# A layer with attention and a dense branch: five and three maxima in the two steps of a chunk of seven products

## The chip, the cores and the metric

The kernel runs on one core of a Trainium2 chip. The metric is the device time of one execution in microseconds (us).

## The reference

The input x has 2048 rows of 512 numbers. Each row is normalized (xn). Then two branches are computed from xn and joined:

```
q = xn @ wq  (32 heads of 16),  k = xn @ wk,  v = xn @ wv   (one head of k and v for all)
p = softmax(q . k / 4)  over all 2048 keys
s = (p @ v, heads side by side) @ wo
h = xn @ w1 + b1            (1792 wide)
g = silu( (h * tanh(softplus(h))) @ w2 )
out = x + s * g
```

Everything is float32, and the softmax subtracts the maximum of a row's scores.

## The kernel before

**Steps.** The queries are worked off in 32 units (`NU`): four blocks of 512 queries, each with eight units of four heads. A unit has 16 steps, one for each 128 keys, so there are 512 steps. In a step TensorE makes four score tiles of 128 keys by 512 queries (`e_one`, line 1030), ScalarE takes their exponentials (line 1032), and two steps later TensorE multiplies them with v (`pv`, line 1104). The maxima that the softmax subtracts belong to later units and run ahead: a step holds four more score products, turned the other way (128 queries by 512 keys, `m_one`, line 1050), and VectorE takes the maximum along each row (line 1054). Once a unit's maxima are complete, `c_rows` turns them into rows of the query tile. All of this is an order written out in the program: instructions reach the engines in the order of emission, and each engine works in that order.

**Dense products.** Between scores and maxima the program puts the products of the dense work: wq, w1, w2 and wo, each value split into a high and a low part so that a product is three matmuls. A group is one tile of 128 by 512 that is summed in the bank `xps`, of which there is one. The groups of the first two thirds of w2 (`m2_groups`, `THIRDS`) have 15 matmuls, those of the last third, wq, w1 and wo have 12. `chunk_size` cuts a group into chunks of at most eight (`XMAX`): 15 becomes 8 and 7, 12 becomes 6 and 6. A chunk takes two steps: each of its matmuls is made as two halves of 64 rows (`half`), in the first step with one half of the TensorE rows, in the second (`second`) with the other. A group ends with the second step of its last chunk; `finish` then has the bank read out, by a copy on ScalarE (first third of w2, line 839; w1, line 770; wq) or by an addition or multiplication on VectorE (`dve` is set; w2's second and last third at line 845, wo).

**Waves.** Scores and maxima contract over at most 64 rows as well, so a step has two sides that run beside each other: the side of the products (`h`), and the other one (`1 - h`). `em(k)` hands out the maxima to the two sides, after the pattern `EM` = "MEMEMEME" (M a maximum, E a score). `m_sides` gives `k // 2` of the four maxima to the side of the scores and the rest to the side of the products, and keeps the two sides within `MLAG` of each other. `waves` (line 634) then emits the two sides in turn: a product, one entry of the other side, the next product and so on. One such pair is called a wave here. With eight products the sides are 8 products, and 4 scores + 4 maxima; with seven they are 7 products + 1 maximum, and 4 scores + 3 maxima; with six, 6 + 1 and 4 + 3. After the waves of a step come the products with v.

**Banks and waits.** Scores rotate through three banks (`ps_e`, tag "e"), maxima through three others (`ps_m`, tag "m"). Between the two steps of a chunk there is a further wait: the first product of the second step waits for the `relay`, the exponential or maximum of an entry emitted with or behind the last product of the first step, because both halves sum in one bank. Where a group ends and VectorE reads its bank, the maxima emitted from the moment when `HOLD` products are left are held back (`held`) and put behind the reading.

The last 20 steps (`LEAD`) have no maxima any more and are emitted by another function, and a lead of some 94 us ahead of the steps follows a planner. Neither has chunks of seven that the change touches.

Of the kernel before, what the change touches and what calls it, by code (L numbers as in the profile page):

```python
# [32 lines left out]
NU = 8 * NC  # L33
# [9 lines left out]
HOLD = 1  # L43
# [4 lines left out]
MLAG = 4  # L48
# [76 lines left out]
def block_kernel(ctx: ExitStack, tc: tile.TileContext, x, wq, wk, wv, wo, w1, b1, w2, out):  # L125
# [3 lines left out]
    ps_e = ctx.enter_context(tc.tile_pool(name="ps_e", bufs=3, space=bass.MemoryType.PSUM))  # L129
    ps_m = ctx.enter_context(tc.tile_pool(name="ps_m", bufs=3, space=bass.MemoryType.PSUM))  # L130
# [8 lines left out]
    lead = {}  # L139
# [140 lines left out]
    xp_of = {}  # L280
# [209 lines left out]
    cur = {"g": None, "ps": None, "n": 0, "chunk": [], "relay": None}  # L490
# [10 lines left out]
    def begin():  # L501
        prepare()
        if qqueue and is_ready(qqueue[0]):
            g = qqueue.popleft()
        elif queue and is_ready(queue[0]):
            g = queue.popleft()
        else:
            n = next((n for n, g in enumerate(queue) if g.wo is None), None)
            if not n or not is_ready(queue[n]) or queue[n].m1 is None:
                return False  # L510
            g = queue[n]
            del queue[n]
        if g.start:
            g.start()
        if g.alloc:
            ps = g.alloc()
        else:
            ps = ps_x.tile([P, 512], F32, tag="x", name="xps")
        cur.update(g=g, n=0, ps=ps, chunk=[], relay=None)
        return True  # L520

    def finish():
        g = cur["g"]
        if cur["n"] < len(g.mms):
            return False
        for i in g.items:
            i.users -= 1
        cur["g"] = None
        evacs[0] += g.dve
        if lead:  # L530
            lead["post"](g, cur["ps"])
        else:
            g.post(cur["ps"])
            g.done = step[0]
        return True
# [95 lines left out]
    def chunk_size(n):  # L631
        return -(-n // -(-n // XMAX)) if n else 0

    def waves(h, em, new):

        if not cur["chunk"] and (not new or cur["g"] is None and not begin()):
            mms = []  # L640
        else:
            g = cur["g"]
            mms = cur["chunk"] or g.mms[cur["n"]:cur["n"] + chunk_size(len(g.mms) - cur["n"])]
        second = bool(cur["chunk"])
        k = len(mms)
        ms = em(k)
        a = deque(ms[1 - h])
        b = deque(ms[h])
        ps = cur["ps"]
        ends = second and cur["n"] + k == len(cur["g"].mms)  # L650
        xs = deque(mms)
        relay = None
        first = True
        done = False
        while a or b or xs:
            if xs:
                i = xs.popleft().half(ps, h)
                if first and cur["relay"] is not None:
                    tc.add_manual_dep(i.ins, cur["relay"].ins.name, mybir.DependencyInfo(
                        mybir.DependencyClass.Sync, mybir.DependencyReason.DATA), reason="other half of the bank")  # L660
                first = False
                if ends and cur["g"].dve and len(xs) == HOLD:
                    held[0] = []
                if not xs and ends:
                    cur["n"] += k
                    cur["chunk"] = []
                    finish()
                    done = True
                    for top in held[0] or ():
                        top()  # L670
                    held[0] = None
            elif b:
                b.popleft()()
            if len(a) > 1 or a and not xs:
                r = a.popleft()()
                if k and not xs and relay is None:
                    relay = r
        if k and not done:
            assert relay is not None
            cur["relay"] = relay  # L680
            if second:
                cur["n"] += k
                cur["chunk"] = []
            else:
                cur["chunk"] = mms
# [308 lines left out]
    for c in range(NC):  # L994
        for k in range(3):
            a = take(2)
# [38 lines left out]

    m_next = [0, 0]

    def m_one(a):
        v, n = MSEQ[m_next[a]] if m_next[a] < 64 else divmod(m_next[a], 32)
        m_next[a] += 1  # L1040
        if v not in mb_of:
            mb_of[v] = sb.tile([P, 4, 16], F32, tag="mb", name=f"mb{v}", bufs=2)
        q = qt_of[v]
        kb, j = divmod(n, 8)
        p, t = divmod(j, 4)
        o = 64 * a
        ps, tag = (ps_e, "e") if lead and 15 in xp_of and a else (ps_m, "m")
        m = ps.tile([P, C], F32, tag=tag, name=f"m{v}_{a}_{n}")
        o = slice(o, o + (HALF if v < len(qts) else 48))
        pe.matmul(m, q[o, p, P * t:P * (t + 1)], ks[o, C * kb:C * (kb + 1)], start=True, stop=True)  # L1050
        z = 8 * a + 4 * p + t

        def top():
            return dve.reduce_max(out=mb_of[v][:, kb, z:z + 1], in_=m, axis=AX.X)  # L1054
        if held[0] is None:
            return top()
        held[0].append(top)

    def m_sides(h, n):

        ahead = m_next[h] - m_next[1 - h]
        lo = max((4 - MLAG - ahead + 1) // 2, 4 - (32 * NU - m_next[1 - h]))
        hi = min((4 + MLAG - ahead) // 2, 32 * NU - m_next[h])
        return max(min(n, hi), lo)

    def c_rows(v):

# [203 lines left out]
    for c0, c1 in ((0, 1), (1, 2), (2, 3), (3, 4)):  # L1271
# [4 lines left out]
        for c in range(c0, c1):  # L1276
            xs, scs = [], []
            for t in range(4 * c, 4 * c + 4):
# [3 lines left out]
                if c == 0:  # L1282
                    hi = task("ACT", 0.55, lambda t=t: x_high(t), [tr])
                    lo = task("DVE", 0.65, lambda t=t: x_low(t), [hi])
# [5 lines left out]
                else:  # L1290
                    lo = task("ACT", 0.62, lambda t=t: x_copy(t), [tr])
# [65 lines left out]
    while True:  # L1357
# [7 lines left out]
        b = best("PE")  # L1365
        m = m_ready(T["PE"])
        if m is not None and b and b[0] < T["PE"] + 0.2 and T["DVE"] > T["PE"] + 1.0:
            m = None
# [10 lines left out]
        s, e, k = min(opts, key=lambda o: o[0])  # L1379
# [5 lines left out]
        if k == "M":  # L1385
# [7 lines left out]
            if vdone[0] == 0 and min(m_next) >= m_need(0):  # L1393
                vdone[0] = 1
                r = c_rows(0)
# [18 lines left out]
        elif k == "J":  # L1414
            tag = next((g for g in ("wq", "ws", "wb") if (g == "wq" or s > 19.0) and arrived(g) and busy[0] + E0 < s + 0.5), None)
            n = ran[0]
# [16 lines left out]
    while left:  # L1433
        k = next(k for k in left if all(d.end is not None for d in k.deps))
# [18 lines left out]
    for s in range(NS + 2000):  # L1453
        inm = s < NS - LEAD
        if inm or cur["chunk"]:
            assert s < NS
            due(s)
            h = s % 2

            def em(k):  # L1460
                n = m_sides(1 - h, k // 2) if inm else 0
                x = deque(lambda i=i: e_one(s, i) for i in range(4))
                y = deque(lambda: m_one(1 - h) for _ in range(n))
                r = [[], []]
                for op in EM:
                    if op == "M" and y:
                        r[1 - h].append(y.popleft())
                    elif op == "E":
                        r[1 - h].append(x.popleft())
                r[h] = [lambda: m_one(h) for _ in range(4 - n if inm else 0)]  # L1470
                return r

            if s >= 2 and (s - 1) % 16 == 0 and s > 1:
                gap[0] += 1
            waves(h, em, inm)
            act_jobs(1 + (len(jobs) > 2))
            due(s + 0.5)
            pv_to(s - 2)
        elif s < NS:
            due(s)  # L1480
            if not late_banks:
                late_banks.extend(ps_m.tile([P, C], F32, tag="m", name=f"late{k}") for k in range(3))
                if (NS - s) % 2:
                    for i in range(4):
                        e_one(s, i)
                    fill(4)
                    act_jobs(1)
                    pv_to(s - 2)
                    step[0] = s
                    continue  # L1490
            if (NS - s) % 2 == 0:
                late_pair(s)
            else:
                act_jobs(1)
                pv_to(s - 1)
        else:
            due(s)
            pv_to(NS - 1)
            act_jobs(100)
            lanes_end()  # L1500
            due(s + 0.5)
            fill(16)
        step[0] = s
        if vdone[0] < 8 * NC and min(m_next) >= m_need(vdone[0]):
            r = c_rows(vdone[0])
            rowq.extend([r[0], lambda r=r: (r[1](), r[2](), r[3]())])
            vdone[0] += 1
        if rowq and not evacs[0]:
            rowq.popleft()()
        evacs[0] = 0  # L1510
        pump()
        if s > NS + 1 and not queue and cur["g"] is None and not timed and not jobs:
            break
# [12 lines left out]
```

## Time and profile before

| | us |
|---|---|
| median of 3 runs | 1590.27 (1589.85 to 1590.56) |
| profiled execution | 1596.07 |
| span of the profiled execution | 1594.3 |

| engine | busy, us | share of the span |
|---|---|---|
| TensorE (matmuls) | 1579.1 | 99% |
| TensorE (weight loads) | 842.3 | 53% |
| VectorE | 1346.8 | 84% |
| ScalarE | 1306.9 | 82% |
| GpSimd | 629.4 | 39% |

In the rows of the profile PE is TensorE's matmuls, PEld its weight loads, DVE VectorE, ACT ScalarE, POOL GpSimd, SP the queue that issues DMAs. A row of the timeline gives the start and the duration in us, the engine, the line, the operation, and what is written and read: `e` is a score bank, `m` a bank of a maximum, `xps` the bank of the dense sum, `pt` an exponential, `mb` the maxima, `pv` the product with v. Behind them stands in brackets how long the engine sat idle, and what ended that. xN says that N neighbouring instructions are merged in one row. A step begins with the load of its first product, which is the `xps` load with some 0.84 us of idle time ahead of it (the loads of the products with v are through early).

### The profile page before, as it was taken

How to read it: one execution, taken by the hardware profiler on the slowest of the kernel's cores; microseconds unless marked ns; L12 is line 12 of the kernel's file. 1: busy time of each engine (PE TensorE's matmuls, PEld its weight loads, DVE VectorE, ACT ScalarE, POOL GpSimd, SP SyncE). 2: the span in 40 equal slices, each digit the busy share in tenths (PEclk: the TensorE clock that was granted, in tenths of full speed). 3: DMA queues.
4: the chain of work that ended last, by engine and by line, in shares of the span. 5: the costliest groups of instructions: out<-in, count | busy, mean ns of one | idle time of the engine just before them, and what ended most of it. 6: DMA issues, size and time to landing. Idle time of an engine off the chain costs nothing.

```text
span 1594.3 us, 31628 instructions
## 1 busy us (share of the span) xinstructions
PE 1579.1 (99%) x11708; PEld 842.3 (53%) x11708; DVE 1346.8 (84%) x2335; ACT 1306.9 (82%) x2515; POOL 629.4 (39%) x643
## 2 busy tenths in 40 slices
PE   9999999999999999999999999999999999999998
PEld 5455555555555455555555555555555555555554
DVE  8888888888989888888898988888889998888832
ACT  7478788798898778978989787897898878789876
POOL 3477166265464104613425221362252414226413
PEclk9899999999999999999999999999999999999999
DMA  6233131142331304112122321220332213031020
GB/s 193 93 103 124 41 111 50 44 137 84 94 118 35 112 18 150 58 52 82 37 67 86 86 82 44 96 70 18 123 97 84 67 59 97 17 110 58 9 87 28
DMA packets 74666, 124.31 MB, mean 78 GB/s; under 512 B 21520, under 2 KB 35344, under 8 KB 74512
## 3 DMA queue, kind: packets, MB, share of 16 engines
q1 hardware_dynamic: 74512, 122.29, 24.7%
q8 instruction: 93, 1.52, 0.4%
q14 instruction: 61, 0.50, 0.1%
HBM read 74.78 MB, written 26.21 MB: 63 GB/s over the span
## 4 chain that ended last, share of the span: by engine, by line
PE 96%; DVE 2%; ACT 1%; DMA 1%; SPq 0%; issue 0%; POOL 0%; DVEq 0%
PE xps L118 46%; PE pv L1104 32%; PE m L1050 8%; PE e L1030 6%; PE xps L114 1%; DVE mb L1054 1%; PE kp L319 1%; ACT pt L1032 0%; DMA wbs<-w 0%; PE late L118 0%; DMA xin<-in_dram 0%; PE xp L287 0%; PE late L1030 0%; PE wop L118 0%; DVE xt L162 0%
## 5 line engine op out<-in xcount | busy, mean ns | idle before, releaser
L1054 DVE TENSOR_REDUCE mb<-m 128x1 f32<-128x512 f32 x2048 | 1271.4, 682 | 178.1 <-PE m L1050 142.0
L1032 ACT ACTIVATE pt<-e 128x512 f32<-128x512 f32 x2019 | 1061.7, 602 | 227.9 <-PE e L1030 222.0
L1050 PE MATMUL m<-ks,qt 48*128 48x512 f32 (+1 forms) x2048 | 847.9, 424 | 2.1 <-DVE ks L237 1.1
L1030 PE MATMUL e<-qt,ks 64*128 64x512 f32 x2019 | 736.5, 401 | 1.0 <-ACT pt L1032 1.0
L1104 PE MATMUL pv<-pt,vaug 128*32 128x512 f32 x4096 | 543.2, 604 | 0.0
L1050 PEld LDWEIGHTS m<-ks,qt 48*128 48x128 f32 (+1 forms) x2048 | 373.9, 186 | 65.4 <-DVE mb L1054 31.8
L1030 PEld LDWEIGHTS e<-qt,ks 64*128 64x128 f32 x2019 | 372.8, 186 | 15.9 <-ACT pt L1032 8.5
L118 PE MATMUL xps<-wbs,act 64*128 64x512 f32 x1240 | 336.2, 407 | 1.3 <-DMA wbs<-w 1.3
L118 PEld LDWEIGHTS xps<-wbs,act 64*128 64x128 f32 x1240 | 216.1, 185 | 177.4 <-ACT pt L1032 105.7
L118 PE MATMUL xps<-xt,ws 64*128 64x512 f32 x1104 | 305.8, 410 | 0.3 <-DVE y L845 0.3
L118 PEld LDWEIGHTS xps<-xt,ws 64*128 64x128 f32 x1104 | 190.2, 185 | 182.8 <-ACT pt L1032 121.6
L172 POOL TENSOR_SCALAR t<-t 128x512 f32<-128x512 f32 x56 | 34.5, 616 | 326.8 <-ACT t L778 326.5
L1104 PEld LDWEIGHTS pv<-pt,vaug 128*32 128x32 f32 x4096 | 81.7, 108 | 143.9 <-issue 134.7
L162 POOL TENSOR_TENSOR hb<-hb,t 128x512 f32<-128x512 f32 x56 | 72.2, 1289 | 68.3 <-ACT t L791 46.8
L118 PE MATMUL xps<-xt,wq 64*128 64x512 f32 x336 | 93.1, 410 | 0.0
L118 PEld LDWEIGHTS xps<-xt,wq 64*128 64x128 f32 x336 | 57.9, 185 | 55.6 <-ACT pt L1032 35.2
L118 PE MATMUL xps<-wbs,ot_all 64*128 64x512 f32 x288 | 79.5, 408 | 0.0
L118 PEld LDWEIGHTS xps<-wbs,ot_all 64*128 64x128 f32 x288 | 49.5, 184 | 47.0 <-ACT pt L1032 31.9
L162 POOL TENSOR_TENSOR hb<-hb,u 128x512 f32<-128x512 f32 x56 | 72.3, 1291 | 4.4
L162 POOL TENSOR_TENSOR u<-u,t 128x512 f32<-128x512 f32 x56 | 71.8, 1282 | 4.7
L162 POOL TENSOR_TENSOR act<-hb,act 128x512 fp32r<-128x512 f32 x55 | 70.8, 1288 | 4.6
L162 POOL TENSOR_TENSOR oc<-oc,sc 128x512 f32<-128x512 f32 (+1 forms) x16 | 20.6, 1287 | 120.7 <-ACT sc L1132 52.9
(144 smaller groups left out, 955.5 us busy)
## 6 DMA issues: line engine op xcount, KB each, us to landing
wbs<-w SPq DMA_DIRECT2D x36, 512.0 KB
ws<-w SPq DMA_DIRECT2D x35, 512.0 KB
qt<-qh SPq DMA_DIRECT2D x256, 32.0 KB
wq<-wq SPq DMA_DIRECT2D x14, 512.0 KB
w<-wbs SPq DMA_DIRECT2D x14, 512.0 KB
wbs<-wo SPq DMA_DIRECT2D x12, 512.0 KB
rawws<-in_dram SPq DMA_DIRECT2D x21, 256.0 KB
rawwb<-in_dram SPq DMA_DIRECT2D x20, 256.0 KB
```

What stands on the lines that cost most here:

```text
L114: return self.pe.matmul(ps, self.lhs(), self.rhs(), start=(self.k == 0), stop=(self.k == self.tot - 1))
L118: i = self.pe.matmul(ps, self.lhs()[o], self.rhs()[o], start=(self.k == 0 and self.halves == 0), stop=(self.k == self.tot - 1 and self.hal ...
L162: eng.tensor_tensor(out=o, in0=a, in1=b, op=op)
L172: pool.tensor_scalar(o, o, lim, 0.0, op0=ALU.min, op1=ALU.max)
L319: pe.matmul(kp_of[c], wkf[:, dt], xf_of[c][dt // 2][:, dt % 2], start=(dt == 0), stop=(dt == 3))
L1030: pe.matmul(e, ks[o:o + 64, P * k:P * (k + 1)], q[o:o + 64, p], start=True, stop=True)
L1032: r = act.activation(pt, e, AF.Exp, scale=0.25)
L1050: pe.matmul(m, q[o, p, P * t:P * (t + 1)], ks[o, C * kb:C * (kb + 1)], start=True, stop=True)
L1054: return dve.reduce_max(out=mb_of[v][:, kb, z:z + 1], in_=m, axis=AX.X)
L1104: pe.matmul(o[32 * j:32 * j + 32], vaug[:, k], pt, start=(k == 0), stop=(k == 15))
```

## The change

It touches only steps whose chunk has an odd number of products, which are those of seven. The two steps of such a chunk have eight maxima together, before and after. Before they are four and four, after it five and three (`tot` in `m_sides`). In the first step the side of the scores gets four maxima and four scores, and the side of the products its seven products and, as the last thing of the step (`swap`), the fifth maximum; that one is put into a score bank (`other`), behind the fourth score. The relay of that step is the fourth exponential. In the second step the side of the scores has four scores and three maxima, and the side of the products has its seven products alone. Where VectorE reads the bank at the end of the group, maxima are held back from the moment when two products are left, not one (`HOLD + k % 2`).

```diff
@@ waves
-        ms = em(k)
+        ms = em(k, second)
...
+        swap = k % 2 and not second
...
-                if ends and cur["g"].dve and len(xs) == HOLD:
+                if ends and cur["g"].dve and len(xs) == HOLD + k % 2:
                     held[0] = []
...
-            elif b:
+            elif b and not swap:
                 b.popleft()()
             if len(a) > 1 or a and not xs:
                 r = a.popleft()()
-                if k and not xs and relay is None:
+                if k and not xs and relay is None and not (swap and a):
                     relay = r
+            if b and swap and not xs and not a:
+                b.popleft()()
@@ m_one
-    def m_one(a):
+    def m_one(a, other=False):
...
-        ps, tag = (ps_e, "e") if lead and 15 in xp_of and a else (ps_m, "m")
+        ps, tag = (ps_e, "e") if other or lead and 15 in xp_of and a else (ps_m, "m")
@@ m_sides
-    def m_sides(h, n):
-
+    def m_sides(h, k, second):
+
+        tot = 4 + (0 if k % 2 == 0 else -1 if second else 1)
+        tot = min(tot, 64 * NU - sum(m_next))
         ahead = m_next[h] - m_next[1 - h]
-        lo = max((4 - MLAG - ahead + 1) // 2, 4 - (32 * NU - m_next[1 - h]))
-        hi = min((4 + MLAG - ahead) // 2, 32 * NU - m_next[h])
-        return max(min(n, hi), lo)
+        lo = max((tot - MLAG - ahead + 1) // 2, tot - (32 * NU - m_next[1 - h]), 0)
+        hi = min((tot + MLAG - ahead) // 2, 32 * NU - m_next[h], tot)
+        n = max(min((k + tot - 4) // 2 if k % 2 else k // 2, hi), lo)
+        return n, tot - n
@@ em
-            def em(k):
-                n = m_sides(1 - h, k // 2) if inm else 0
+            def em(k, second):
+                n, rest = m_sides(1 - h, k, second) if inm else (0, 0)
...
-                r[h] = [lambda: m_one(h) for _ in range(4 - n if inm else 0)]
+                r[h] = [lambda j=j: m_one(h, n + rest > 4 and j == rest - 1) for j in range(rest)]
```

## The prediction

> **What bounds the kernel now.** I read the page's busy shares, then its chain and its groups, and after that the timeline of single engines, one step at a time.
>
> ```profile
> span 1594.3 us, 31628 instructions
> PE 1579.1 (99%) x11708; PEld 842.3 (53%) x11708; DVE 1346.8 (84%) x2335; ACT 1306.9 (82%) x2515; POOL 629.4 (39%) x643
> PE 96%; DVE 2%; ACT 1%; DMA 1%; SPq 0%; issue 0%; POOL 0%; DVEq 0%
> L1054 DVE TENSOR_REDUCE mb<-m 128x1 f32<-128x512 f32 x2048 | 1271.4, 682 | 178.1 <-PE m L1050 142.0
> ```
>
> TensorE is busy 99% of the span and is 96% of the chain; VectorE, which reads the maxima, has idle time before them. So a step lasts as long as its matmuls take, unless one of them waits for a bank. The weight loads show the order inside a step best, because a load carries the wait for its bank. Here is a pair of steps with seven products, first and second:
>
> ```profile
> 1095.03 0.18 PEld L118 LDWEIGHTS xps<-wbs,act 64*128 64x128 f32 x1 [0.84 <-ACT pt L1032]
> ...
> 1096.31 0.18 PEld L118 LDWEIGHTS xps<-wbs,act 64*128 64x128 f32 x1
> 1096.46 0.18 PEld L1030 LDWEIGHTS e<-qt,ks 64*128 64x128 f32 x1
> 1096.55 0.18 PEld L1050 LDWEIGHTS m<-ks,qt 48*128 48x128 f32 x1
> 1097.09 0.16 PEld L1104 LDWEIGHTS pv<-pt,vaug 128*32 128x32 f32 x8 [0.36 <-issue]
> 1098.09 0.18 PEld L118 LDWEIGHTS xps<-wbs,act 64*128 64x128 f32 x1 [0.84 <-ACT pt L1032]
> ...
> 1101.19 0.18 PEld L118 LDWEIGHTS xps<-xt,wq 64*128 64x128 f32 x1 [0.89 <-DVE y L845]
> ```
>
> The first step runs from 1095.03 to 1098.09, 3.05 us, the second to 1101.19, 3.10 us. In each, the seven products on one half of the rows stand beside four scores and three maxima on the other half; the fourth maximum (1096.55) is alone in an eighth wave. A step with six products has only seven waves:
>
> ```profile
> 1106.91 0.18 PEld L118 LDWEIGHTS xps<-xt,wq 64*128 64x128 f32 x1 [0.84 <-ACT pt L1032]
> 1109.76 0.18 PEld L118 LDWEIGHTS xps<-xt,wq 64*128 64x128 f32 x1 [0.84 <-ACT pt L1032]
> ```
>
> That is 2.85 us, so a wave less is worth 0.20 us. This is what the change is after: fifteen waves in a pair, not sixteen. Reading all step starts I find 31 such pairs before the closing steps. 16 end with ScalarE's copy of the sum, 15 with VectorE's addition.
>
> **The second step, with three maxima.** The lone maximum goes, and seven waves are left, 2.85 us. Whether the next group can begin then depends on when its only bank, xps, has been read out.
>
> ```profile
> L839 ACT ACTIVATE y<-xps x16: 603/603/617, 142.6 to 1402.7; 128x512 f32<-128x512 f32 x16
> ```
>
> ```profile
> 1376.64 0.18 PEld L118 LDWEIGHTS xps<-wbs,act 64*128 64x128 f32 x1 [0.84 <-ACT pt L1032]
> ...
> 1379.69 0.18 PEld L118 LDWEIGHTS xps<-xt,wq 64*128 64x128 f32 x1 [0.84 <-ACT y L839]
> ```
>
> ```profile
> 1378.92 0.60 ACT L839 ACTIVATE y<-xps 128x512 f32<-128x512 f32 x1
> ```
>
> ScalarE's copy stands behind the third exponential in its queue and ends at 1379.52, 2.88 us into the step. So far that was hidden, as the step lasted 3.05. With seven waves the next product is due at 2.85 and must wait for the copy, and with 0.05 us for the release (the price is read below) begins at 2.93. The gain is 0.12 us, not 0.20, in 16 pairs: -1.9 us.
>
> ```profile
> 1098.65 1.89 DVE L1054 TENSOR_REDUCE mb<-m 128x1 f32<-128x512 f32 x3 [0.57 <-PE m L1050]
> 1100.45 0.68 DVE L845 TENSOR_TENSOR y<-xps,y 128x512 f32<-128x512 f32 x1
> 1101.05 1.37 DVE L1054 TENSOR_REDUCE mb<-m 128x1 f32<-128x512 f32 x2
> ```
>
> Where VectorE adds, the addition follows three maxima and ends at 1101.13, and the next product began 0.06 later. The change holds the third maximum back too (HOLD + 1), so the addition follows two. It can begin when the seventh product is through, 1.90 us into the step and a few hundredths on, and ends near 2.65, before 2.85 us. The full 0.25 us is gained in 15 pairs: -3.8 us. The held maximum then ends near 3.25, 0.4 into the next step, while VectorE idles for the first 0.57 of a step. If that cover were gone, the next first maximum would slip by the overrun, and a bank of the three with it.
>
> **The first step, with five maxima.** Products and scores now fill eight waves as in a step with eight products, so the count of waves stays. The new element is the fifth maximum in wave eight, behind the fourth score, on the ring of three score banks. The trace of before has no maximum on a score bank in a step, but it shows the ring: the fourth score needs the bank of the first.
>
> ```profile
> 1095.81 0.60 ACT L1032 ACTIVATE pt<-e 128x512 f32<-128x512 f32 x1 [0.95 <-PE e L1030]
> ```
>
> ```profile
> 1096.34 0.60 ACT L1032 ACTIVATE pt<-e 128x512 f32<-128x512 f32 x1
> ```
>
> The first exponential ends at 1096.41 and the fourth score's load starts at 1096.46: 0.05 us from release to load. By the same ring the fifth maximum needs the bank of the second score, whose exponential (1096.34) ends only at 1096.94, 1.91 us into the step. Its load should start near 1.51, as the lone maximum's did (1096.55), to be in time for wave eight. It will start at 1.96 instead, and behind it on TensorE's queue stand the context products (pv) and then the whole second step. What such a late last matmul costs is shown by a step with six products whose fourth score was late:
>
> ```profile
> 241.08 0.61 ACT L1032 ACTIVATE pt<-e 128x512 f32<-128x512 f32 x1
> ```
>
> ```profile
> 241.74 0.18 PEld L1030 LDWEIGHTS e<-qt,ks 64*128 64x128 f32 x1 [0.17 <-ACT pt L1032]
> 242.17 0.16 PEld L1104 LDWEIGHTS pv<-pt,vaug 128*32 128x32 f32 x8 [0.25 <-issue]
> 243.17 0.18 PEld L118 LDWEIGHTS xps<-xt,early 64*128 64x128 f32 x1 [0.84 <-ACT pt L1032]
> ```
>
> From the end of the exponential (241.69) to the next step's first product are 1.48 us. So the first step becomes 1.91 + 1.48 = 3.38 us, 0.33 more than now. In about a third of the 31 first steps the second exponential ends earlier, as here:
>
> ```profile
> 1082.77 0.18 PEld L118 LDWEIGHTS xps<-wbs,act 64*128 64x128 f32 x1 [0.84 <-ACT pt L1032]
> ```
>
> ```profile
> 1084.04 0.59 ACT L1032 ACTIVATE pt<-e 128x512 f32<-128x512 f32 x1
> ```
>
> It ends 1.86 us in, and the loss is 0.29. I take 0.32 as the mean, with bounds of 0.29 and 0.35. One of the 31 costs nothing:
>
> ```profile
> 553.77 0.49 PE L118 MATMUL xps<-wbs,act 64*128 64x512 f32 x1
> ...
> 556.25 0.50 PE L118 MATMUL xps<-wbs,act 64*128 64x512 f32 x1 [1.27 <-DMA wbs<-w]
> ```
>
> There weights come late, and the second exponential is long over before wave eight. That leaves 30 x 0.32 = +9.6 us.
>
> [...] The row: in the late case the load and its matmul begin together, and the matmul's record is longer than the usual 0.39.
>
> ```profile
> 241.74 0.50 PE L1030 MATMUL e<-qt,ks 64*128 64x512 f32 x1
> 242.17 0.64 PE L1104 MATMUL pv<-pt,vaug 128*32 128x512 f32 x4
> ```
>
> About 0.11 us of weight load is thus exposed, which is inside the 1.48. [...]
>
> **VectorE and the rest.** Five maxima fit:
>
> ```profile
> 1361.92 2.48 DVE L1054 TENSOR_REDUCE mb<-m 128x1 f32<-128x512 f32 x4 [0.59 <-PE m L1050]
> ```
>
> Four take 2.48 us, 0.62 each, and this step began at 1361.35: the fourth ends 3.05 in, the fifth 3.67, which is 0.3 into a second step that starts at 3.38. Its first maximum needs VectorE at 0.57; the third score, which takes the fifth maximum's bank, is due past 1.0. Both are covered, so I cost them at nothing. The relay (the first product of the second step waits for the fourth exponential, now a wave later) is covered as well: that exponential ends near 2.9. No DMA and no GpSimd instruction moves, and the maxima of a pair stay eight, so the row constants come due in the same steps.
>
> **Sum.** +9.6 - 1.9 - 3.8 = +3.9 us. The profiled execution took 1596.07 us around its span of 1594.3, the median of the runs is 1590.27; I add 3.9 to each: 1600.0 and 1594.2. With 0.29 to 0.35 us in the first step and 0.10 to 0.20 where ScalarE copies, the forecast alone goes from +1.7 to +5.1, 1592.0 to 1595.4.
>
> **Rivals.** (a) The bank is free in time and the fifth maximum costs nothing; the pairs then give back 5.7 us: 1584.6, faster. The deciding point is in wave eight of the first step: with 30 first steps against 5.7 us, the break-even loss is 0.19, so the second exponential would have to end by 1.77 us, and for the full gain by 1.46. For it speaks that ScalarE has idle time; against it that the earliest end I found is 1.86, set by the score's own wave and not by a queue. Chance 0.09.
> (b) The exposed load is hidden: 30 x 0.21 = 6.3 less 5.7, +0.6 us, 1590.9, no change. [...] Chance 0.05.
> (c) The change does not do in the second step what it says: VectorE's addition still comes behind three maxima, the next product begins at 3.10 as now, and only the copies' 1.9 us are gained: +7.7, 1598.0. For it speaks that held maxima are counted by hand; against it that the fifth product lies just ahead of the third maximum in the order. Chance 0.10.
>
> **How the numbers follow.** The forecast keeps 0.76. About 0.2% (3.2 us) is what a measurement of this kernel can tell from no change. The forecast's 3.9 stands only 0.7 above it, so I put 0.55 of its 0.76 above and 0.21 within. With (c) slower is 0.65, with (b) same is 0.26, faster 0.09. The range reaches from (b) to (c), 1590.8 to 1598.0, and leaves out (a) and thin tails.
>
> **What would show it.** In the profile after: first steps of 3.34 to 3.38 us, with the last L1050 load of the step ended by ACT pt near 1.96 us; second steps of 2.93 us ended by ACT y and of 2.85 where VectorE adds; the total idle time that L1050's loads spend on ScalarE's exponentials rising from about nothing to some 30 x 0.25 us (1.96 less the 1.70 at which the fourth score's load is through). I am wrong if the first steps stay at 3.05 us (a), or if the second steps with an addition stay above 3.0 (c).

## The result, and the profile after

Over 21 runs each, the median went from 1590.9 to 1595.6 us. The ratio of the changed kernel to the one before is 1.0024, 95% interval [1.0015, 1.0033]: some 3.8 us more (2.4 to 5.2 by the interval), slower, as forecast. The two medians lie 4.7 us apart, because a run's time also moves with its lead, which took 88.1 to 94.1 us in the profiled executions (last section).

The page of the kernel after shows almost nothing of it. TensorE is as full as before, and the span of this one execution is even shorter than that of before:

```profile
span 1592.2 us, 31628 instructions
PE 1576.9 (99%) x11708; PEld 841.0 (53%) x11708; DVE 1347.2 (85%) x2335; ACT 1306.6 (82%) x2515; POOL 629.0 (40%) x643
```

So the steps have to be cut out of the span. The two fences below are from the timelines of the weight loads, before and then after: the first step behind the lead, and the step after the last pair of seven.

```profile
94.11 0.18 PEld L118 LDWEIGHTS xps<-xt,early 64*128 64x128 f32 x1 [0.84 <-ACT pt L1032]
...
1520.88 0.18 PEld L118 LDWEIGHTS xps<-wbs,act 64*128 64x128 f32 x1 [0.89 <-DVE y L845]
```

```profile
88.54 0.18 PEld L118 LDWEIGHTS xps<-xt,early 64*128 64x128 f32 x1 [0.84 <-ACT pt L1035]
...
1518.79 0.18 PEld L118 LDWEIGHTS xps<-wbs,act 64*128 64x128 f32 x1 [0.84 <-DVE y L848]
```

Between them lie 1426.77 us before and 1430.25 after: the steps take 3.5 us more. The lead, which the change does not touch, took 5.6 us less in this execution; the last section says why.

Here is the pair that was shown of before, in the kernel after (its lines 1053 and 1033 are the maxima and scores that stood at 1050 and 1030; 1035, 842, 848 and 1057 were 1032, 839, 845 and 1054):

```profile
1091.86 0.18 PEld L118 LDWEIGHTS xps<-wbs,act 64*128 64x128 f32 x1 [0.84 <-ACT pt L1035]
...
1093.39 0.19 PEld L1033 LDWEIGHTS e<-qt,ks 64*128 64x128 f32 x1
1093.82 0.18 PEld L1053 LDWEIGHTS m<-ks,qt 48*128 48x128 f32 x1 [0.24 <-ACT pt L1035]
1094.24 0.16 PEld L1110 LDWEIGHTS pv<-pt,vaug 128*32 128x32 f32 x8 [0.24 <-issue]
1095.24 0.18 PEld L118 LDWEIGHTS xps<-wbs,act 64*128 64x128 f32 x1 [0.84 <-ACT pt L1035]
...
1098.09 0.18 PEld L118 LDWEIGHTS xps<-xt,wq 64*128 64x128 f32 x1 [0.84 <-DVE y L848]
```

The fifth maximum's load comes at 1093.82, 1.96 us into the step, after idle time that ScalarE ended. The first step lasts 3.38 us where it lasted 3.05, the second 2.85 where it lasted 3.10. ScalarE's timeline has the exponential it waited for, the second score's:

```profile
1093.17 0.60 ACT L1035 ACTIVATE pt<-e 128x512 f32<-128x512 f32 x1
```

It ends at 1093.77, and the load follows 0.05 us later. The list of waits (engine, line, what was waited for: us in total, times, longest) has, next to the maxima's waits for VectorE, a line for this that the list of before lacks, the second one here:

```profile
PEld m L1053 <- DVE mb L1057: 29.5, 78, 0.8
PEld m L1053 <- ACT pt L1035: 6.7, 29, 0.3
```

Second steps that end with ScalarE's copy, such as this one, take 2.94 us, and the idle time ahead of the next product is 0.93 us, above the 0.84 that stands ahead of the other steps shown here:

```profile
1374.31 0.18 PEld L118 LDWEIGHTS xps<-wbs,act 64*128 64x128 f32 x1 [0.84 <-ACT pt L1035]
...
1377.25 0.18 PEld L118 LDWEIGHTS xps<-xt,wq 64*128 64x128 f32 x1 [0.93 <-ACT y L842]
```

In second steps that end with VectorE's addition, the addition now follows two maxima. This is VectorE in the second step of the pair above:

```profile
1095.81 1.29 DVE L1057 TENSOR_REDUCE mb<-m 128x1 f32<-128x512 f32 x2 [0.30 <-PE xps L118]
1097.28 0.69 DVE L848 TENSOR_TENSOR y<-xps,y 128x512 f32<-128x512 f32 x1 [0.18 <-PE e L1033]
1097.89 0.68 DVE L1057 TENSOR_REDUCE mb<-m 128x1 f32<-128x512 f32 x1
```

From all step starts, read out in this way, come the figures of this table: the median length of the steps of seven, in us, and how the steps together (between the two starts above) stand to the kernel before.

| kernel | first steps (31) | second, copy (16) | second, addition (15) | all steps, against before |
|---|---|---|---|---|
| before | 3.05 | 3.05 | 3.10 | |
| after | 3.37 | 2.94 | 2.85 | +3.5 |
| e1, fifth on a bank of the maxima | 3.33 | 2.94 | 2.85 | +2.2 |
| e2, hold as before | 3.38 | 2.94 | 3.11 | +7.8 |
| e3, half of the second exponential | 3.16 | 2.93 | 2.85 | +9.2 (see there) |
| e4, first step begins with a score | 3.14 | 2.93 | 2.85 | -2.2 |
| e5, both steps begin with a score | 3.15 | 2.83 | 2.83 | -4.3 |
| e6, as e4, fifth on a bank of the maxima | 3.57 | 2.94 | 2.85 | +9.9 |

Steps of six and of eight products kept their medians (2.85 and 3.07 us before) within 0.01 us in all of these kernels.

### The profile page after: what moved, and what is told of

The parts are those of the page before. It is cut to its first block, busy times and chain, and to the rows that moved or that the text cites. A ratio compares the mean times of both kernels' runs of the same rounds, so it can differ in the third digit from the quotient of the medians.

```text
span 1592.2 us, 31628 instructions
## 1 busy us (share of the span) xinstructions
PE 1576.9 (99%) x11708; PEld 841.0 (53%) x11708; DVE 1347.2 (85%) x2335; ACT 1306.6 (82%) x2515; POOL 629.0 (40%) x643
## 4 chain that ended last, share of the span: by engine, by line
PE 96%; DVE 2%; ACT 1%; DMA 0%; issue 0%; POOL 0%; SPq 0%; DVEq 0%
PE xps L118 45%; PE pv L1110 32%; PE m L1053 8%; PE e L1033 8%; PE xps L114 1%; PE kp L319 1%; DVE mb L1057 1%; ACT pt L1035 1%; PE warm L1261 1%; DMA wbs<-w 0%; PE xp L287 0%; PE wop L118 0%; PE late L118 0%; PE late L1033 0%; DVE xt L162 0%
```

## The experiments

The theory: the first step lasts 1.48 us from the moment at which the bank of its last matmul comes free, and that is when the second score's exponential ends. The rivals: VectorE, with five maxima, sets that step; or the taking of a score bank costs by itself, through the scores behind it; or the relay (the fourth exponential) sets the start of the second step. Each edit is against the kernel after, unless it says otherwise. The kernels e1, e2, e3 and e6 were run once, and their step lengths are what is compared; e4 and e5 were timed as well.

**e1: another ring for the fifth maximum.**

```diff
-        ps, tag = (ps_e, "e") if other or lead and 15 in xp_of and a else (ps_m, "m")
+        ps, tag = (ps_e, "e") if lead and 15 in xp_of and a else (ps_m, "m")
```

> The fifth maximum takes a bank of the maxima's ring, so it needs the bank of the second maximum instead of the second score. Theory (the first step lasts 1.48 us from the release of the bank that the last matmul needs): VectorE has read the second maximum 1.85 us into the step in the changed kernel, so the first steps take 3.33 us, 0.04 less than there (3.37), now ended by VectorE; the rest stays, about 1.1 us less in all. Rival 1 (VectorE's load of five maxima sets the first step): same first steps, 3.37. Rival 2 (taking a score bank is what costs, through the scores behind it): first steps fall to 3.05.

The pair's first step in the timeline of the weight loads:

```profile
1095.60 0.18 PEld L118 LDWEIGHTS xps<-wbs,act 64*128 64x128 f32 x1 [0.84 <-ACT pt L1035]
...
1097.51 0.18 PEld L1053 LDWEIGHTS m<-ks,qt 48*128 48x128 f32 x1 [0.20 <-DVE mb L1057]
...
1098.93 0.18 PEld L118 LDWEIGHTS xps<-wbs,act 64*128 64x128 f32 x1 [0.84 <-ACT pt L1035]
```

3.33 us, and the load now waits for VectorE; all steps together are 1.3 us shorter than in the kernel after, where 1.1 were expected. The wait follows the bank. With the score banks free of the fifth maximum the step did not return to 3.05, so taking a score bank is not what costs. VectorE's load alone is not ruled out by this run.

**e2: hold back maxima as late as before.**

```diff
-                if ends and cur["g"].dve and len(xs) == HOLD + k % 2:
+                if ends and cur["g"].dve and len(xs) == HOLD:
```

> The maxima are held back only when one product is left, as before the change. Theory (VectorE's addition is early because it stands behind two maxima): the 15 second steps that end with an addition go back from 2.85 to 3.10 us, and nothing else changes: +3.8 us against the changed kernel. Rival (those steps are shorter because of the missing wave alone): they stay at 2.85.

VectorE's timeline in that pair's second step, then the next step's first load:

```profile
1100.74 1.89 DVE L1057 TENSOR_REDUCE mb<-m 128x1 f32<-128x512 f32 x3 [0.30 <-PE m L1053]
1102.54 0.68 DVE L848 TENSOR_TENSOR y<-xps,y 128x512 f32<-128x512 f32 x1
```

```profile
1103.27 0.18 PEld L118 LDWEIGHTS xps<-xt,wq 64*128 64x128 f32 x1 [1.09 <-DVE y L848]
```

The addition is behind three maxima again, ends at 1103.22, and the next product begins 0.05 us after. The medians went from 2.85 to 3.11 us, +4.3 us for all steps against the kernel after, where 3.8 were expected. The excess lies in two pairs in which the row constants stand on VectorE as well. The missing wave alone gives nothing here: it pays only with the earlier place of the addition in VectorE's queue.

**e3: a shorter second exponential.**

```diff
-        r = act.activation(pt, e, AF.Exp, scale=0.25)
+        w = slice(0, C // 2 if half else C)
+        r = act.activation(pt[:, w], e[:, w], AF.Exp, scale=0.25)
+        if half:
+            pool.memset(pt[:, C // 2:], 0.25)
```

Here `half` is true for the second score of a pair's first step.

> In the first step of each pair the second score's exponential covers 256 of its 512 columns (the other half of that tile is set to a constant by GpSimd, so part of the softmax is left out). VectorE's five maxima are untouched. Theory (the fifth maximum waits for that exponential): copies of 256 columns elsewhere took about 0.38 us on ScalarE where 512 took 0.60, so the bank comes free 0.21 us earlier and the first steps fall from 3.37 to about 3.16 us, 30 x 0.21 = 6.3 us less in all. Rival 1 (VectorE's load of five maxima): first steps stay at 3.37. Rival 2 (the fourth exponential, on which the second step's first product waits, sets it): about the same fall would come only if the whole queue of exponentials moved, and the wait would be seen at the products, not at the fifth maximum's load.

ScalarE's first two exponentials of that pair's first step in one row, and two loads, of the fifth maximum and of the second step's first product:

```profile
1101.63 0.92 ACT L1036 ACTIVATE pt<-e 128x512 f32<-128x512 f32 x2 [0.95 <-PE e L1033]
```

```profile
1102.60 0.18 PEld L1056 LDWEIGHTS m<-ks,qt 48*128 48x128 f32 x1
...
1104.03 0.18 PEld L118 LDWEIGHTS xps<-wbs,act 64*128 64x128 f32 x1 [0.84 <-ACT pt L1036]
```

The second ends at 1102.55, and the fifth maximum is loaded 0.05 us later. The median of the first steps is 3.16 us, as forecast, with VectorE's five maxima as they were, and the 31 first steps together are 7.0 us shorter than in the kernel after (105.5 to 98.6). That speaks for the exponential and against VectorE. It speaks against the relay too: the fourth exponential ends 2.80 us into these steps (median), only 0.08 earlier than in the kernel after, while the steps got 0.21 shorter. That the bracket of the second step's first load names an exponential of ScalarE in either kernel does not tell what set the step. The steps in all did not get shorter, though, which was not expected: two second steps, at 670.7 and 955.3 us, last 7.1 and 7.7 us in this kernel. In both, the constant that GpSimd writes stood behind its other work, and the products with v waited for it, 3.8 us each time. The list of waits has the two:

```profile
PEld pv L1113 <- POOL pt L1038: 7.7, 2, 3.8
```

With each of these waits TensorE's granted clock fell to half, for 3.4 and 6.8 us (in the row below, a stretch of 2 us, it is the figure after GpSimd's, 0.50), and the steps of eight products that followed took 4.27 and 4.98 us, not 3.07. So the loss in all steps comes from the constant, which is this edit's own, and says nothing of the change.

```profile
678.00:680.00 2.00, 2.00 (x10) 1.60 (x12) 1.12 (x2) 0.60 (x1) 1.72 (x2) 0.50 0.00 0
```

**e4: begin the first step with a score.**

```diff
-                if k and not xs and relay is None and not (swap and a):
+                if k and not xs and relay is None:
...
-                for op in EM:
+                for op in ("EMEMEMEM" if k % 2 and not second else EM):
```

> In the first step of a pair the side of the scores begins with a score, not a maximum (E M E M E M E M), and the relay is again the entry that goes with the last product (the fourth score). Theory: the second score is a wave earlier, its exponential ends near 1.65 us, the fifth maximum's load starts at 1.70 and the first steps take 1.65 + 1.48 = 3.13 us; second steps as in the changed kernel (2.93 and 2.85). Sum against the kernel before: 31 x 0.08 - 1.9 - 3.8 = -3.2 us, ratio 0.998. Rival 1 (VectorE's five maxima): they start a wave later, so the first steps get longer, 3.37 to 3.6, ratio 1.002 to 1.007. Rival 2 (any fifth entry on the score ring costs about 0.3 us): unchanged, ratio 1.0024.

The first step began at 1088.50. The second exponential in ScalarE's timeline, and the second step's first load:

```profile
1089.57 0.60 ACT L1035 ACTIVATE pt<-e 128x512 f32<-128x512 f32 x1
```

```profile
1091.64 0.18 PEld L118 LDWEIGHTS xps<-wbs,act 64*128 64x128 f32 x1 [0.84 <-ACT pt L1035]
```

The exponential ends 1.67 us into the step, and the step takes 3.14 (expected 3.13). VectorE reads its five maxima later here than in the kernel after (the fifth is through 3.88 us into the step, not 3.65), and still the step is 0.23 us shorter. With e3 this settles the rival. The steps together take 2.2 us less than before, not 3.2. The missing 1.0 lies in two second steps, both with the row constants (`c_rows`) on VectorE between the fifth maximum and the addition. Here is one, by the loads of its own and of the next step's first product:

```profile
1474.74 0.18 PEld L118 LDWEIGHTS xps<-wbs,act 64*128 64x128 f32 x1 [0.84 <-ACT pt L1035]
...
1478.42 0.18 PEld L118 LDWEIGHTS xps<-xt,ws 64*128 64x128 f32 x1 [1.67 <-DVE y L848]
```

It takes 3.68 us, where the kernel after took 3.21; the other went from 2.85 to 3.32. The ratio to the kernel before was 0.9993 [0.9980, 1.0005]: no difference that the timing can tell, so e4's gain is read from the steps alone.

**e5: begin both steps with a score.**

```diff
-                for op in ("EMEMEMEM" if k % 2 and not second else EM):
+                for op in ("EMEMEMEM" if k % 2 else EM):
```

This edit is against e4.

> As e4_scores_first, and the second step of a pair begins with a score too. Theory: the third exponential then ends near 2.15 us into the second step and ScalarE's copy of the sum near 2.63, before the next product is due, so the 16 second steps with a copy fall from 2.93 to 2.85 us, 1.3 us less than e4_scores_first; the first steps stay at 3.14. Steps in all about 3.5 us shorter than before, ratio 0.998. Rival (the 2.93 us come from something else than the copy's place in ScalarE's queue): second steps stay at 2.93. Risk by the theory: the third score of the second step needs the fifth maximum's bank, which VectorE frees some 0.75 us into the step, and its load is due at 0.82.

ScalarE's copy in the second step that begins at 1370.74, and the next step's first load:

```profile
1372.79 0.60 ACT L842 ACTIVATE y<-xps 128x512 f32<-128x512 f32 x1
```

```profile
1373.57 0.18 PEld L118 LDWEIGHTS xps<-xt,wq 64*128 64x128 f32 x1 [0.84 <-ACT y L842]
```

The copy ends 2.65 us into the step, the wait is back to 0.84, and the step takes 2.83 us: the 2.93 came from the copy's place behind the third exponential. The risk that was named, the third score's bank, did not show: that load came 0.82 us into the step, when it was due. The steps take 4.3 us less than before (3.5 were expected; the second steps fell to 2.83, not 2.85, those with an addition too), and the ratio to the kernel before is 0.9972 [0.9959, 0.9985]. So this version is faster than the kernel before, by some 0.3%. It was not timed beside the kernel after; its steps are 7.8 us shorter than there.

**e6: scores first, but the fifth maximum on a bank of the maxima.**

```diff
-        ps, tag = (ps_e, "e") if other or lead and 15 in xp_of and a else (ps_m, "m")
+        ps, tag = (ps_e, "e") if lead and 15 in xp_of and a else (ps_m, "m")
```

This edit, too, is against e4.

> As e4_scores_first, but the fifth maximum takes a bank of the maxima's ring. Theory: with scores first the second maximum is read out only at 2.09 us, so the first steps take 2.09 + 1.48 = 3.57 us, 0.43 more than in e4_scores_first, ended by VectorE. Rival (a score at the head of the step is what helps, whatever bank the fifth maximum has): 3.14.

```profile
1097.83 0.18 PEld L1053 LDWEIGHTS m<-ks,qt 48*128 48x128 f32 x1 [0.41 <-DVE mb L1057]
```

This load of the fifth maximum comes 2.15 us into its step (which began at 1095.68), and the median of the first steps is 3.57 us. The fourth exponential ends 2.65 us into the step here and in e4 alike, so the relay does not set it. So a score at the head helps only by way of the bank that the last matmul needs. The same order of waves gives 3.14 or 3.57 us, by which bank the last one takes.

## Why the prediction was right

The prediction had the cost, the two gains and their causes right. Its three terms can be summed over the step starts of the two traces.

| term | forecast | measured |
|---|---|---|
| first steps | +9.6 | +9.25 |
| second steps with a copy | -1.9 | -1.9 |
| second steps with an addition | -3.8 | -3.8 |
| sum | +3.9 | +3.5 |

- *First step.* The late six-product step of before, 1.48 us from the end of an exponential to the next step, was the right pattern: in the kernels after, e1, e3, e4 and e6 the release stood at 1.90, 1.85, 1.69, 1.67 and 2.09 us (medians) and the step ended 1.47 to 1.48 us later each time. In the pair of the kernel after these are 0.05 us to the load of the last matmul, 0.42 to the first product with v, and 1.00 for the eight of them. The waits of the fifth maxima for ScalarE come to 6.7 us in 29 steps, where some 7.5 in 30 were forecast. That the fifth maximum takes the second score's bank, worked out from the ring, is shown by e3 and e1. The step at 553.77 with its late weights cost nothing, as said: 4.61 us before, 4.55 after.
- *Second step with a copy.* The forecast of 2.93 was 2.94; e5 shows the reason.
- *Second step with an addition.* 2.85 came as forecast, and e2 shows that it hangs on HOLD. The addition began 0.14 us after the seventh product was through (1.90 us into the step), not a few hundredths, and ended at 2.73 in the pair shown, not near 2.65. That this cost nothing is in part luck: 0.07 us more, with 0.05 for the release, would have reached 2.85.
- *Covers.* VectorE's fifth maximum and the relay were costed at nothing. That held, but in the two pairs with row constants and an addition little of the cover is left: with the maxima a wave later, e4 lost 0.47 us in each of them.
- *Rivals.* (a), the bank free in time, and (c), the addition behind three maxima, did not come. The break-even of (a), a second exponential that ends by 1.77 us, is borne out by e4's steps: with 1.67 the same division of maxima takes 2.2 us less than before. (b), the hidden weight load, did not come either: the load at 1093.82 started only when the bank was free, its matmul began with it, and that matmul's record is 0.49 us long, where the others of this step behind its first wave have 0.39 or 0.40.
- *The profiled execution.* 1600.0 us was forecast for it and 1593.93 was measured. The error is not in a step; it was wrong to take the lead as the same in every execution. For the median 1594.2 was forecast, on a median of 1590.27 before; the 21 runs gave 1590.9 before and 1595.6 after.

## What to carry to other kernels

When a matmul is moved onto another ring of banks, count back through the ring to find whose reader it waits for, and put the end of that reader beside the time at which the load has to start; a wave saved elsewhere can be smaller than this wait (here it gave 0.11 us in the second steps with a copy, and the wait cost 0.32 in the first steps). In this kernel the remedy was not another bank (e1, 3.33 us) but the order ahead of it: one swap (a score before a maximum) brought the release forward by 0.23 us in the first steps and turned the 3.5 us that the steps took more than before into 2.2 less, and the same swap in the second steps made it 4.3 less. Where a step gets shorter, look for the reader that was hidden at its end, and for its place in its engine's queue.

## What the runs showed of the hardware

The lead of some 90 us took between 88.1 and 94.1 us in the profiled executions, though TensorE's instructions there are the same (before and after, 333 matmuls and 333 weight loads ahead of the first step). The cause is seen in the granted clock (the column after POOL's, in stretches of 4 us; the mean over the whole span, 0.994 before and 0.999 after, hides it). Before, and then after:

```profile
62.00:66.00 4.00, 3.03 (x14) 1.91 (x15) 3.41 (x7) 0.25 (x1) 1.27 (x1) 0.91 0.24 68
66.00:70.00 4.00, 3.94 (x10) 1.60 (x9) 3.65 (x8) 1.84 (x3) 1.59 (x3) 0.50 0.00 0
...
78.00:82.00 4.00, 4.00 (x12) 2.32 (x10) 2.63 (x5) 0.52 (x1) 3.88 (x4) 0.50 0.03 5
82.00:86.00 4.00, 3.65 (x16) 1.83 (x16) 2.61 (x5) 1.32 (x2) 1.95 (x3) 0.96 0.31 91
```

```profile
78.00:82.00 4.00, 3.59 (x18) 1.84 (x16) 4.00 (x8) 2.11 (x4) 3.75 (x5) 1.00 0.29 84
82.00:86.00 4.00, 3.58 (x17) 2.31 (x18) 3.61 (x6) 2.49 (x5) 3.83 (x5) 0.58 0.04 10
```

In the execution of before TensorE ran at half its clock for some 17.1 us of the lead, in that of after for 3.4, in that of e6 not at all. Over the eight executions the lead goes with it: 88.1 us with none, 88.5 and 89.5 with 3.4, 90.2 with 6.8, 90.8 to 93.4 with 10.2, and 94.1 with 17.1. When it began before, 3.03 of 4 us were busy, and no gap in that stretch was longer than 1.14 us; the step at 553.77, with 2.73 of 4 us busy and a gap of 1.27, kept the full clock. The two falls of the clock in e3's steps came with pauses of 2.9 us. The lengths, 3.4, 6.8, 10.2 and 17.1 us, are close to one, two, three and five times the shortest. What sets the half clock off is not shown by these rows and was not tried. The runs' times go with the mean granted clock: in one series of before the runs at 0.994 took 1594.9 to 1596.0 us and those at 0.999 and 1.000 1589.3 to 1589.9. So a change of this size has to be read from the steps, or from many runs.
